# A fused attention and expert kernel on one core: the router summed in PSUM by thirds, even expert capacities, a slot table in four parts

## The chip, the cores and the metric

The kernel runs on one core of a Trainium2 chip. The metric is the time of one execution in microseconds on the device; lower is better. The kernel before takes 606.49 us, the median of three runs (604.68 to 609.28).

## What is computed

Two stages follow each other: windowed attention over 8 batches of 8 heads with 576 positions of width 64, and a mixture of 16 experts (4 groups of 4) over the 4608 tokens that come out of it. Each token goes to one expert, the best of its best group, and its output is weighted by the two softmax values.

```python
# attention: x[token, 512], from windows of 32 keys (half of the heads with a stride of 4)
g_logits = x @ w_group                      # 4 groups
g_idx = argmax(g_logits); g_w = softmax(g_logits)[g_idx]
for g in range(4):
    xg = x[g_idx == g]
    e_logits = xg @ w_expert[g]             # 4 experts in the group
    e_idx = argmax(e_logits); e_w = softmax(e_logits)[e_idx]
    for e in range(4):
        h = maximum(xg[e_idx == e] @ w1[g, e], 0)      # 512 -> 1024
        out[those tokens] = g_w * e_w * (h @ w2[g, e])  # 1024 -> 512
```

## The kernel before

**Attention.** The loop over `s` runs 36 steps of 128 queries and three more that empty its pipeline. A step holds on TensorE (PE): the scores (L266, L278), the transposes of the probabilities of the step before (L301), the product with the values of the step before that (L311), and the transposes of finished rows into `xT` (L363). ScalarE (ACT) takes the exponentials (`p`, L294) and copies out of PSUM; VectorE (DVE) takes the row maxima, differences and normalisation (L288, L289, L339); GpSimd (POOL) shifts the values (L125, L131). Inputs and the finished rows (`xd`) move by DMAs on SyncE's queue.

**Router.** The steps are nine to a pair of batches, 1152 tokens (9 tiles of 128). When a pair is done, `route(bp)` runs beside the attention steps of the next pair: a generator whose pieces are handed out by `spend`, at most 1.8 us of estimated work a step, and which stops for a step where a piece yields 2. So its matmuls over the tokens (L380) stand in one step and the sums of the logits (L391) in the next. The model width of 512 is cut into four row blocks `c`. The first matmuls write block `c` of a third of the tokens to partitions 32c of a PSUM tile, ACT copies each third to `lt` (L387), and nine matmuls against `sumsel` (four stacked unit matrices of 20 columns, L391) add the four blocks and turn the tokens into partitions. DVE then finds group and expert (L396 to L435), matmuls with a triangle of ones count the ranks (L444, L446), and each token gets a slot.

**Slot table.** `tab` holds for every slot of every expert the token, its weight and its row in `xd`. Each 128 tokens multiply a one-hot matrix of the slot's low part (`ohl`, made on ACT, L246 and L247) with `mv`: the one-hot of its high part times the values (`parts`, L502 on DVE; every third tile in the first three routes on POOL, L494 and L495). The three values are split into two fp16 parts each, so `mv` has 6 x 64 columns, multiplied in two matmuls of 192 columns that add into the same PSUM (`tb_ps`, L521). Then `tab` takes the sum (L531), and `select` (L684, L691) and `unpack` (L655 to L657) take an expert's slots out of it.

**Experts.** Expert ranks by size have fixed capacities `CAPS`. Slots past a capacity go through a loop at the end, of no rounds where all fit. Three early pieces of the two largest experts start before routing is done. `layer1` runs 8 x 12 matmuls whose moving side is as wide as the piece (L750), `layer2` 24 matmuls of 512 columns for each tile of 128 rows (L809; a last tile of up to 64 or 32 rows is cut into two or four side by side). Rows come by gathers on POOL (L700) and leave by scatters (L770).

**Order.** In the attention stage PE, ACT, DVE and SyncE take the order of the program as written. After it the string `TAIL` sets by hand how the fourth route, the early pieces and the weights of the second expert alternate. There `R` runs the fourth route up to its first stop, `r` one piece of it.

Of the kernel before, what the change touches and what calls it, by code (L numbers as in the profile page):

```python
# [17 lines left out]
P = 128  # L18
# [15 lines left out]
R256 = 1.5 * 2.0**31  # L34
# [5 lines left out]
CAPS = (448, 408, 368, 304, 304, 304, 296, 288, 272, 264, 256, 256, 248, 240, 216, 192)  # L40
# [17 lines left out]
NCHK = NTOK // P  # L58
NK4 = 4
# [5 lines left out]
def moe_attention_kernel(ctx, tc, q, k, v, cmask, wgate, wpack, out):  # L65
# [89 lines left out]
    wgr = cp.tile([P, 128 + NCHK], F32, name="wgr")  # L155
    wg = wgr[:, 0:128].rearrange("p (c n) -> p c n", c=4)
    sumsel = cp.tile([P, 20], F32, name="sumsel")
# [15 lines left out]
    parts = cp.tile([P, NCHK, 6], F16, name="parts")  # L173
# [9 lines left out]
    def setup(part):  # L183
        if part == 0:
            nc.vector.memset(ones, 1.0)
            nc.gpsimd.affine_select(
                out=upper, in_=ones, pattern=[[1, P]], compare_op=ALU.is_gt, fill=0.0, base=0, channel_multiplier=-1
            )
            nc.sync.dma_start(wgr, wgate)
            nc.vector.tensor_copy(sumsel, id32[:, 0:20])  # L190
            for c in range(1, 4):
                nc.vector.tensor_tensor(sumsel, sumsel, id32[:, 32 * c : 32 * c + 20], ALU.add)
            iota_of(pri, [[-1, 4]], 4, 0)
            iota_of(base[0], [[REG, NE]], 0, 0)
            iota_of(low, [[1, P]], 0, 0)
        if part == 1:
            iota_of(val[:, :, 0], [[P, NCHK]], -NTOK, 1)
            iota_of(parts[:, :, 0], [[P, NCHK]], -NTOK, 0)
            iota_of(parts[:, :, 3], [[0, NCHK]], 0, 1)
# [3 lines left out]
            nc.vector.memset(tab[:, 0], float(NTOK))  # L203
            nc.vector.memset(tab[:, 1], 0.0)
            nc.vector.memset(tab[:, 2], 2.0 * NTOK + 1.0)
            nc.vector.tensor_copy(val[:, :, 2], wgr[:, 128:])
            nc.vector.tensor_scalar(parts[:, :, 2], val[:, :, 2], R256, R256, ALU.add, ALU.subtract)
            nc.vector.tensor_tensor(parts[:, :, 5], val[:, :, 2], parts[:, :, 2], ALU.subtract)
# [161 lines left out]
    def route(bp):  # L370
        lt = sm.tile([P, TPB, P], F32, name="lt")
        TPC = TPB // 3
        for i in range(3):
            ps = (psT, psT, psR)[i].tile([P, TPC * P], F32, name="lt_ps", tag="ttr"[i])
            a0 = i * TPC * P
            cuts = [a0] + [S] * (a0 < S < a0 + TPC * P) + [a0 + TPC * P]
            for a, b in zip(cuts, cuts[1:]):
                bb, s0, n = a // S, a % S, b - a
                for c in range(4):
                    nc.tensor.matmul(  # L380
                        ps[32 * c : 32 * c + 32, a - a0 : b - a0],
                        wg[:, c],
                        xT[bp][:, c, bb, s0 : s0 + n],
                        start=True,
                        stop=True,
                    )
# [88 lines left out]
        nc.vector.reciprocal(val[:, mine, 1], se)  # L475
        yield 0
        nc.vector.tensor_copy(parts[:, mine, 1], val[:, mine, 1])
        yield 0
        nc.vector.tensor_tensor(parts[:, mine, 4], val[:, mine, 1], parts[:, mine, 1], ALU.subtract)
# [4 lines left out]
        for t0 in range(0, n, 3):  # L484
            ohl = sm.tile([P, 3, P], F16, name="ohl", bufs=2)
            mv = sm.tile([P, 3, 6, NE * NK4], F16, name="mv", bufs=2)
            for t in range(3):
# [4 lines left out]
                if last < NBP and t == 2:  # L492
# [4 lines left out]
                        ohh.rearrange("p e k -> p (e k)").unsqueeze(1).broadcast_to([P, 6, NE * NK4]),  # L497
                        parts[:, bp * TPB + t0 + t].unsqueeze(2).broadcast_to([P, 6, NE * NK4]),
# [5 lines left out]
                    high.rearrange("p e k -> p (e k)").unsqueeze(1).broadcast_to([P, 6, NE * NK4]),  # L504
                    hl[:, 1, t0 + t : t0 + t + 1],
                    parts[:, bp * TPB + t0 + t].unsqueeze(2).broadcast_to([P, 6, NE * NK4]),
# [11 lines left out]
            for t1, lo, hv in done:  # L518
                for t in range(3):
                    for h in range(2):  # L520
                        nc.tensor.matmul(  # L521
                            tb_ps,
                            lo[:, t],
                            hv[:, t, 3 * h : 3 * h + 3].rearrange("p v n -> p (v n)"),
                            start=(t1 + t + h == 0),
                            stop=(t1 + t == n - 1 and h == 1),
                        )
# [125 lines left out]
    def unpack(ent, cs, three):  # L653
        n = three.shape[-1]
        nc.vector.tensor_copy(ent[:, 0:3:2, 0:n], three[:, 0:3:2])  # L655
        nc.vector.tensor_scalar(ent[:, 1, 0:n], three[:, 0], 2.0, 0.0, ALU.mult, ALU.add)
        nc.vector.tensor_scalar_mul(cs[:, 0:n], three[:, 1], 1.0 / (SH * SW * SG))  # L657
# [4 lines left out]
    def note_tail(cs, three, cap):  # L662
# [4 lines left out]
        nc.vector.tensor_scalar_add(tq[0:n, 0:1], three[0:n, 0, t : t + 1], -float(NTOK))  # L667
# [446 lines left out]
    with tc.For_i(0, nov, 1) as i:  # L1114
# [11 lines left out]
        nc.vector.tensor_scalar_add(three[:, 0:1], three[:, 0:1], float(NTOK))  # L1126
# [13 lines left out]
def layout(q, k, v, moe_w_group, moe_w_expert, moe_w1, moe_w2):  # L1140
# [37 lines left out]
    wgate = np.concatenate([wgate, 2.0 * (row - NTOK)], axis=1).astype(np.float32)  # L1178
# [26 lines left out]
```

## Time and profile before

| | us |
|---|---|
| median of three runs (lowest to highest) | 606.49 (604.68 to 609.28) |
| the profiled execution | 609.38 |
| its span, first to last instruction | 607.7 |
| busy in the span: PE, PE's weight loads, DVE, ACT, POOL | 571.0, 400.4, 395.1, 329.5, 247.7 |
| mean granted TensorE clock | 0.982 of full |

The profiled execution lies 1.7 us above its span and 2.9 us above the median. Matmuls are pipelined, so PE's busy time counts waits inside the array too. Shares of the whole span mix stages with different limits. A PE clock of 1.00 is 2.4 GHz, one of 0.50 is 1.2 GHz.

### The profile page before, as it was taken

How to read it: one execution, taken by the hardware profiler on the slowest of the kernel's cores; microseconds unless marked ns; L12 is line 12 of the kernel's file. 1: busy time of each engine (PE TensorE's matmuls, PEld its weight loads, DVE VectorE, ACT ScalarE, POOL GpSimd, SP SyncE). 2: the span in 40 equal slices, each digit the busy share in tenths (PEclk: the TensorE clock that was granted, in tenths of full speed). 3: DMA queues.
4: the chain of work that ended last, by engine and by line, in shares of the span. 5: the costliest groups of instructions: out<-in, count | busy, mean ns of one | idle time of the engine just before them, and what ended most of it. 6: DMA issues, size and time to landing. Idle time of an engine off the chain costs nothing.

```text
span 607.7 us, 18716 instructions
## 1 busy us (share of the span) xinstructions
PE 571.0 (94%) x7636; PEld 400.4 (66%) x7636; DVE 395.1 (65%) x800; ACT 329.5 (54%) x658; POOL 247.7 (41%) x314
## 2 busy tenths in 40 slices
PE   5898999988879999999999999999999999999995
PEld 3665776666666668665666575666757767767873
DVE  5764874897957853774778786655755666656720
ACT  2555674675566533774465555465655756656521
POOL 4754582655726324143425151433524413413411
PEclk9999998989989999999999999999999999999999
DMA  7998796799374118676567576757668578677300
GB/s 245 298 287 262 238 277 185 237 356 335 71 250 144 51 47 318 219 259 205 183 198 223 187 229 205 226 175 232 209 211 258 180 243 275 227 233 254 103 30 29
DMA packets 47914, 127.52 MB, mean 210 GB/s; under 512 B 7224, under 2 KB 8126, under 8 KB 47826
## 3 DMA queue, kind: packets, MB, share of 16 engines
q1 hardware_dynamic: 40466, 105.31, 54.9%
q0 software_dynamic: 7360, 20.98, 9.8%
q8 instruction: 62, 1.02, 0.7%
q14 instruction: 26, 0.21, 0.1%
HBM read 107.38 MB, written 19.24 MB: 208 GB/s over the span
## 4 chain that ended last, share of the span: by engine, by line
PE 65%; issue 3%; DVE 2%; POOL 1%; ACT 1%; POOLq 0%
PE y L809 31%; PE a L750 30%; PE pt L731 3%; DVE mv L502 1%; POOL xe L700 1%; PE tb_ps L521 0%; POOL out L770 0%; PE rp L676 0%; ACT off L246 0%; DVE room L758 0%; ACT xT L367 0%; ACT ohl L247 0%; PE o L311 0%; ACT room L757 0%; DVE room L733 0%
## 5 line engine op out<-in xcount | busy, mean ns | idle before, releaser
L700 POOL DMA_INDIRECT xr<-xd,sent x80 | 96.1, 1201 | 35.2 <-issue 22.2
L809 PEld LDWEIGHTS <-hh 128*128 128x128 f16 (+10 forms) x960 | 67.5, 99 | 58.0 <-issue 2.9
L770 POOL DMA_INDIRECT out<-yr,sent x30 | 30.2, 1007 | 180.2 <-ACT yr L783 148.0
L758 DVE SCALAR_TENSOR_TENSOR hl<-a,hh 128x256 f16<-128x256 f32 (+11 forms) x136 | 57.3, 424 | 65.9 <-ACT hh L757 64.8
L757 ACT ACTIVATE hh<-a 128x256 f16<-128x256 f32 (+11 forms) x136 | 51.9, 385 | 51.9 <-PE a L750 51.2
L750 PE MATMUL a<-xh,wb1h 128*128 128x256 f16 (+6 forms) x288 | 77.0, 271 | 0.0
L750 PE MATMUL a<-xl,wb1h 128*128 128x256 f16 (+6 forms) x288 | 77.0, 271 | 0.0
L750 PE MATMUL a<-xh,wb1l 128*128 128x256 f16 (+6 forms) x288 | 77.0, 271 | 0.0
L733 DVE TENSOR_TENSOR xl<-pt,xh 128x512 f16<-128x512 f32 (+10 forms) x42 | 24.8, 594 | 73.5 <-ACT xh L732 73.5
L750 PE MATMUL a<-xh,wa1h 128*128 128x192 f16 (+7 forms) x256 | 71.2, 278 | 0.0
L750 PE MATMUL a<-xh,wa1l 128*128 128x192 f16 (+7 forms) x256 | 71.2, 278 | 0.0
L750 PE MATMUL a<-xl,wa1h 128*128 128x192 f16 (+7 forms) x256 | 71.2, 278 | 0.0
L783 ACT ACTIVATE yr<-y,cs 128x512 f32<-128x512 f32 (+3 forms) x30 | 20.6, 687 | 90.1 <-PE y L809 61.9
L750 PEld LDWEIGHTS <-wa1h 128*128 128x128 f16 x640 | 59.3, 98 | 13.4 <-issue 1.8
L750 PEld LDWEIGHTS <-wb1h 128*128 128x128 f16 x576 | 54.4, 98 | 10.0
L809 PE MATMUL y<-wb2h,hh 128*128 128x512 f16 (+6 forms) x272 | 59.7, 305 | 0.0
L809 PE MATMUL y<-wb2l,hh 128*128 128x512 f16 (+6 forms) x272 | 59.6, 304 | 0.0
L809 PE MATMUL y<-wb2h,hl 128*128 128x512 f16 (+6 forms) x272 | 59.6, 304 | 0.0
L809 PE MATMUL y<-wa2h,hh 128*128 128x512 f16 (+7 forms) x208 | 56.8, 332 | 0.0
L809 PE MATMUL y<-wa2l,hh 128*128 128x512 f16 (+7 forms) x208 | 56.6, 330 | 0.0
L809 PE MATMUL y<-wa2h,hl 128*128 128x512 f16 (+7 forms) x208 | 56.6, 330 | 0.0
L809 PEld LDWEIGHTS <-hl 128*128 128x128 f16 (+10 forms) x480 | 34.6, 99 | 25.2
(190 smaller groups left out, 1255.4 us busy)
## 6 DMA issues: line engine op xcount, KB each, us to landing
w<-wpack SPq DMA_DIRECT2D x128, 512.0 KB, 3.9
vt<-v SPq DMA_DIRECT2D x36, 260.0 KB, 4.8
qb<-q SPq DMA_DIRECT2D x36, 256.0 KB, 4.6
xd<-x SPq DMA_DIRECT2D x72, 128.0 KB, 3.9
kr<-k SPq DMA_DIRECT2D x34, 256.0 KB, 4.4
xr<-xd,sent POOLq DMA_INDIRECT x80, 4.1
kr<-k SPq DMA_DIRECT2D x4, 128.0 KB, 3.2
out<-yr,sent POOLq DMA_INDIRECT x30, 2.8
```

The costliest lines, as they stand in the source:

```text
L502: nc.vector.scalar_tensor_tensor(mv[:, t], high.rearrange("p e k -> p (e k)").unsqueeze(1).broadcast_to([P, 6, NE * NK4]), hl[:, 1, t0 + t ...
L700: nc.gpsimd.indirect_dma_start(out=xr[:, 256 * h : 256 * h + 256], out_offset=None, in_=xd[0:known].rearrange("n (h c) -> (n h) c", h=2), ...
L731: nc.tensor.transpose(pt[:, c, 0:n], xr[0:n, c * P : c * P + P], id32[0:n, 0:n])
L733: nc.vector.tensor_tensor(xl[:, :, t * P : t * P + n], pt[:, :, 0:n], xh[:, :, t * P : t * P + n], ALU.subtract)
L750: nc.tensor.matmul(a[:, 0:cap], ww[:, c * FF + f * P : c * FF + f * P + P], xx[:, c, 0:cap], start=(i == 0), stop=(i == len(mm) - 1),)
L757: nc.scalar.activation(hh[:, f, 0:cap], a[:, 0:cap], AF.Relu)
L758: nc.vector.scalar_tensor_tensor(hl[:, f, 0:cap], a[:, 0:cap], 0.0, hh[:, f, 0:cap], ALU.max, ALU.subtract)
L770: ins = nc.gpsimd.indirect_dma_start(out=out.rearrange("n (g c) -> (n g) c", g=g), out_offset=bass.IndirectOffsetOnAxis(ap=at, axis=0), in ...
L783: nc.scalar.activation(yr[0:n, :], yp[0:n, :], AF.Copy, scale=cs[0:n, t : t + 1])
L809: nc.tensor.matmul(yp[P // g * j : P // g * j + n, 0 : DM // g], h[:, f, t * P : t * P + n], ww[:, f * DM + DM // g * j : f * DM + DM // g ...
```

## The change

**Router.** The thirds of the tokens now lie on partitions 0, 32 and 64 of one PSUM tile, and the four row blocks add up in place: `c` is the outer loop, and only the first matmul of a third has `start`. One copy takes 96 partitions to `lt`. Three matmuls against `sel3` (three unit matrices beside each other, 60 columns) give the logits of nine tiles.

**Slot table.** A token's number and its row are coded as even numbers counted back from the end of its pair of batches, from -2304 to -2, which one fp16 holds; only the weight keeps two parts. `mv` has 4 x 64 columns: one matmul of 192 columns and one of 64 per tile. Since the code of all but the last pair is relative, two new DVE instructions (`sh`) take the pair's offset off the entries that were written.

**Capacities.** `CAPS` sums to 4616 instead of 4664.

```diff
-CAPS = (448, 408, 368, 304, 304, 304, 296, 288, 272, 264, 256, 256, 248, 240, 216, 192)
+CAPS = (442, 406, 368, 302, 300, 298, 292, 284, 266, 264, 256, 256, 242, 238, 214, 188)
...
+PAIR2 = 2 * TPB * P
...
-    parts = cp.tile([P, NCHK, 6], F16, name="parts")
+    parts = cp.tile([P, NCHK, 4], F16, name="parts")
...
     def route(bp):
-        lt = sm.tile([P, TPB, P], F32, name="lt")
         TPC = TPB // 3
-        for i in range(3):
-            ps = (psT, psT, psR)[i].tile([P, TPC * P], F32, name="lt_ps", tag="ttr"[i])
-            a0 = i * TPC * P
-            cuts = [a0] + [S] * (a0 < S < a0 + TPC * P) + [a0 + TPC * P]
-            for a, b in zip(cuts, cuts[1:]):
-                bb, s0, n = a // S, a % S, b - a
-                for c in range(4):
+        lt = sm.tile([3 * 32, TPC * P], F32, name="lt")
+        ps = psT.tile([P, TPC * P], F32, name="lt_ps", tag="t")
+        for c in range(4):
+            for j in range(3):
+                a0, a1 = j * TPC * P, (j + 1) * TPC * P
+                cuts = [a0] + [S] * (a0 < S < a1) + [a1]
+                for a, b in zip(cuts, cuts[1:]):
+                    bb, s0 = a // S, a % S
                     nc.tensor.matmul(
-                        ps[32 * c : 32 * c + 32, a - a0 : b - a0],
+                        ps[32 * j : 32 * j + 32, a - a0 : b - a0],
                         wg[:, c],
-                        xT[bp][:, c, bb, s0 : s0 + n],
-                        start=True,
-                        stop=True,
+                        xT[bp][:, c, bb, s0 : s0 + b - a],
+                        start=(c == 0 and a == a0),
+                        stop=(c == 3 and b == a1),
                     )
-            nc.scalar.copy(lt[:, i * TPC : i * TPC + TPC].rearrange("p t n -> p (t n)"), ps)
+        nc.scalar.copy(lt, ps[0 : 3 * 32])
         yield 2
         lg_ps = psR.tile([P, TPB, 20], F32, name="lg_ps", tag="r")
-        for t in range(TPB):
-            nc.tensor.matmul(lg_ps[:, t], lt[:, t], sumsel, start=True, stop=True)
+        for t in range(TPC):
+            nc.tensor.matmul(
+                lg_ps.rearrange("p (j t) e -> p j t e", t=TPC)[:, :, t],
+                lt[:, t * P : t * P + P],
+                sel3[0 : 3 * 32],
+                start=True,
+                stop=True,
+            )
...
-                    for h in range(2):
+                    for v0, v1 in ((0, 3), (3, 4)):
                         nc.tensor.matmul(
-                            tb_ps,
+                            tb_ps[:, 0 : (v1 - v0) * NE * NK4],
                             lo[:, t],
-                            hv[:, t, 3 * h : 3 * h + 3].rearrange("p v n -> p (v n)"),
...
         tf = tab.rearrange("p v e k -> p (v e k)")
+        if last < NBP:
+            sh = T("sh", [2 * NE * NK4])
+            nc.vector.tensor_scalar(sh, tb_ps[:, NE * NK4 :], 0.0, -float(PAIR2 * (NBP - last)), ALU.is_lt, ALU.mult)
+            yield 0
+            nc.vector.tensor_tensor(tf[:, NE * NK4 :], tf[:, NE * NK4 :], sh, ALU.add)
+            yield 0
         nc.vector.tensor_tensor(tf, tf, tb_ps, ALU.add)
```

The rest follows from the code: set-up instructions for `sel3`, `parts` and `tab`, the order of the three values in `unpack`, `note_tail` and the closing loop, and 36 more columns in the table `wgate` that the host lays out.

On PE, in the attention step after the first pair of batches, this stood ahead of the step's transposes (`lt_ps` are the router's first sums, `tx` the transposes of finished rows, `s` the scores):

```order
L380 MATMUL lt_ps<-xT,wgr 32x384 x4
L380 MATMUL lt_ps<-xT,wgr 32x192 x8
L380 MATMUL lt_ps<-xT,wgr 32x384 x4
L363 MATMUL tx<-id_73,x 128x128 x4
L266 LDWEIGHTS idb
L266 MATMUL s<-masks,idb 128x512
```

and now stands this:

```order
L377 MATMUL lt_ps<-xT,wgr 32x384
L377 MATMUL lt_ps<-xT,wgr 32x192 x2
L377 MATMUL lt_ps<-xT,wgr 32x384 x2
L377 MATMUL lt_ps<-xT,wgr 32x192 x2
L377 MATMUL lt_ps<-xT,wgr 32x384 x2
L377 MATMUL lt_ps<-xT,wgr 32x192 x2
L377 MATMUL lt_ps<-xT,wgr 32x384 x2
L377 MATMUL lt_ps<-xT,wgr 32x192 x2
L377 MATMUL lt_ps<-xT,wgr 32x384
```

Sixteen matmuls stay sixteen, at the same place. Before, four neighbours went to four quarters of the array's columns; now a third of the tokens stays in one quarter for all four blocks, so that three quarters are in use, and the middle third comes in two halves one behind the other.

On PE, one step later, the logits (`lg_ps`) between the product with the values (`o`) and the same transposes, before:

```order
L311 MATMUL o<-vt,pt_122 32x65
L391 MATMUL lg_ps<-sumsel,lt 128x20 x9
L363 MATMUL tx<-id_73,x 128x128 x4
L266 LDWEIGHTS idb
L266 MATMUL s<-masks,idb 128x512
L278 MATMUL s<-kr,qb 32x128 x16
```

and now:

```order
L308 MATMUL o<-vt,pt_122 32x65
L388 MATMUL lg_ps<-sel_155,lt 128x3x20 x3
L360 MATMUL tx<-id_73,x 128x128 x4
L263 LDWEIGHTS idb
L263 MATMUL s<-masks,idb 128x512
L275 MATMUL s<-kr,qb 32x128 x16
```

Nine matmuls became three; what follows them moved up.

On DVE, at the end of the third route, where the second and third early pieces' slots are taken (`room` are an early piece's hidden values, `ente` its rows), before:

```order
L758 SCALAR_TENSOR_TENSOR room<-a,room 128x128 x4
L531 TENSOR_TENSOR tab<-tab,tb_ps 128x192
L684 TENSOR_TENSOR sel_3921<-tab,top 128x48
L691 TENSOR_REDUCE three_3923<-sel_3921 128x3
L655 CAST ente_183<-three_3923 128x2
```

and now:

```order
L767 SCALAR_TENSOR_TENSOR room<-a,room 128x128 x4
L536 TENSOR_SCALAR sh<-tb_ps 128x128
L538 TENSOR_TENSOR tab<-tab,sh 128x128
L540 TENSOR_TENSOR tab<-tab,tb_ps 128x192
L693 TENSOR_TENSOR sel_3897<-tab,top 128x48
L700 TENSOR_REDUCE three_3899<-sel_3897 128x3
```

Two instructions came in ahead of the table's sum, and the selection waits behind them. On POOL, whose order is left to the scheduler there, the second of two clearings of 128x256 (L1079) moved from behind the six gathers of the early pieces to ahead of them, so that the fourth route's softmax sums follow the gathers at once.

## Rows read from the trace of the kernel before

**Rows 1.** The page: its chain by engine, and the DMA share by slices.
```profile
PE 65%; issue 3%; DVE 2%; POOL 1%; ACT 1%; POOLq 0%
...
DMA  7998796799374118676567576757668578677300
```

**Rows 2.** Chain in order of time, expert stage: start us, us, what (304, 288 columns).
```profile
350.44 6.20 PE a L750 x48
...
404.96 5.88 PE a L750 x48
```

**Rows 3.** ACT's timeline: the exponentials of two attention steps, five steps apart.
```profile
28.57 0.63 ACT L294 ACTIVATE p<-d 128x512 f32<-128x512 f32 x1
...
47.43 0.62 ACT L294 ACTIVATE p<-d 128x512 f32<-128x512 f32 x1
```

**Rows 4.** Stretches: us, busy PE PEld DVE ACT POOL, PEclk, DMA share, GB/s.
```profile
54.90:60.60 5.70, 5.55 (x139) 3.47 (x132) 2.27 (x4) 3.69 (x10) 1.93 (x4) 1.00 0.85 245
60.60:66.40 5.80, 5.75 (x133) 4.76 (x132) 4.34 (x11) 2.47 (x8) 1.52 (x6) 1.00 0.71 219
92.90:100.20 7.30, 6.03 (x139) 3.62 (x132) 2.28 (x4) 3.72 (x10) 0.62 (x1) 1.00 0.70 201
100.20:108.20 8.00, 8.00 (x125) 6.40 (x125) 4.31 (x10) 2.30 (x8) 2.87 (x9) 0.58 0.53 150
140.90:146.80 5.90, 5.59 (x140) 3.54 (x132) 3.57 (x5) 4.49 (x11) 2.73 (x3) 1.00 1.03 373
146.80:153.70 6.90, 6.90 (x134) 5.68 (x134) 5.64 (x12) 3.54 (x9) 5.33 (x10) 0.75 0.60 203
```

**Rows 5.** Timeline, third and fourth route: ACT's copies of two thirds, PE's logits.
```profile
142.28 0.48 ACT L387 COPY lt<-lt_ps 128x384 f32<-128x384 f32 x1 [0.17 <-PE lt_ps L380]
...
142.93 0.48 ACT L387 COPY lt<-lt_ps 128x384 f32<-128x384 f32 x1 [0.17 <-PE lt_ps L380]
...
185.76 2.14 PE L391 MATMUL lg_ps<-sumsel,lt 128*128 128x20 f32 x18
```

**Rows 6.** Timeline of DVE: its waits for the logits, and one for the scores.
```profile
59.13 0.69 DVE L288 TENSOR_REDUCE mx<-s 128x8 f32<-128x512 f32 x1 [3.16 <-PE s L278]
...
62.74 0.35 DVE L396 TENSOR_REDUCE mx<-lg_ps 128x45 f32<-128x180 f32 x1 [1.04 <-PE lg_ps L391]
...
102.70 0.35 DVE L396 TENSOR_REDUCE mx<-lg_ps 128x45 f32<-128x180 f32 x1 [1.42 <-PE lg_ps L391]
...
148.75 0.35 DVE L396 TENSOR_REDUCE mx<-lg_ps 128x45 f32<-128x180 f32 x1 [0.86 <-PE lg_ps L391]
```

**Rows 7.** Groups by form, DVE: busy us, mean ns, idle before and its releasers.
```profile
L502 DVE SCALAR_TENSOR_TENSOR mv<-high,hl,parts 128x384 f16<-128x384 f32 x27 | 20.3, 789 | 0.5 <-PE tb_ps L521 0.4
...
L758 DVE SCALAR_TENSOR_TENSOR hl<-a,hh 128x304 f16<-128x304 f32 x24 | 11.2, 469 | 7.4 <-ACT hh L757 7.4
...
L758 DVE SCALAR_TENSOR_TENSOR hl<-a,hh 128x192 f16<-128x192 f32 x16 | 5.7, 356 | 17.3 <-ACT hh L757 17.3
...
L531 DVE TENSOR_TENSOR tab<-tab,tb_ps 128x192 f32<-128x192 f32 x4 | 1.4, 347 | 0.2 <-PE tb_ps L521 0.2
```

**Rows 8.** The tile `mv`: its writers' shortest, median and longest ns.
```profile
L502 DVE SCALAR_TENSOR_TENSOR mv<-high,hl,parts x27: 602/619/1267, 71.7 to 200.8; 128x384 f16<-128x384 f32 x27
L495 POOL TENSOR_TENSOR mv<-ohh,parts x9: 826/829/1193, 71.8 to 176.8; 128x384 f16<-128x384 f32 x9
```

**Rows 9.** Busy time by stretches, where the first expert's weights come in.
```profile
116.00:124.00 8.00, 6.47 (x218) 4.79 (x214) 7.68 (x15) 7.21 (x19) 7.11 (x11) 1.00 0.98 333
```

**Rows 10.** Timeline of the fourth route, and the tile `mv`: who waited for it.
```profile
191.84 0.33 POOL L1079 MEMSET xT<- 128x256 f32 x1
...
194.37 0.22 DVE L475 RECIPROCAL val<-se 128x9 f32<-128x9 f32 x1 [1.27 <-POOL se L428]
...
197.52 0.33 PE L521 MATMUL tb_ps<-mv,ohl 128*128 128x192 f16 x2 [0.40 <-DVE mv L502]
...
  PE tb_ps L521: 1.8, 6
```

More of the change, by code (lines that the diff above doesn't have):

```diff
@@ L189, in setup @@
             nc.sync.dma_start(wgr, wgate)
-            nc.vector.tensor_copy(sumsel, id32[:, 0:20])
-            for c in range(1, 4):
-                nc.vector.tensor_tensor(sumsel, sumsel, id32[:, 32 * c : 32 * c + 20], ALU.add)
+            for j in range(3):
+                nc.vector.tensor_copy(sel3[:, j], id32[:, 32 * j : 32 * j + 20])
             iota_of(pri, [[-1, 4]], 4, 0)
@@ L202, in setup @@
             nc.vector.memset(E16, 0.0)
-            nc.vector.memset(tab[:, 0], float(NTOK))
-            nc.vector.memset(tab[:, 1], 0.0)
+            nc.vector.memset(tab[:, 0], 0.0)
+            nc.vector.memset(tab[:, 1], 2.0 * NTOK)
             nc.vector.memset(tab[:, 2], 2.0 * NTOK + 1.0)
-            nc.vector.tensor_copy(val[:, :, 2], wgr[:, 128:])
-            nc.vector.tensor_scalar(parts[:, :, 2], val[:, :, 2], R256, R256, ALU.add, ALU.subtract)
-            nc.vector.tensor_tensor(parts[:, :, 5], val[:, :, 2], parts[:, :, 2], ALU.subtract)
+            nc.vector.tensor_copy(val[:, :, 2], wgr[:, 128 : 128 + NCHK])
+            nc.vector.tensor_copy(parts[:, :, 2], wgr[:, 128 + NCHK :])
         if part == 2:
@@ L519, in route @@
                 for t in range(3):
-                    for h in range(2):
+                    for v0, v1 in ((0, 3), (3, 4)):
                         nc.tensor.matmul(
-                            tb_ps,
+                            tb_ps[:, 0 : (v1 - v0) * NE * NK4],
                             lo[:, t],
-                            hv[:, t, 3 * h : 3 * h + 3].rearrange("p v n -> p (v n)"),
-                            start=(t1 + t + h == 0),
-                            stop=(t1 + t == n - 1 and h == 1),
+                            hv[:, t, v0:v1].rearrange("p v n -> p (v n)"),
+                            start=(t1 + t + v0 == 0),
+                            stop=(t1 + t == n - 1 and v0 == 3),
                         )
@@ L654, in unpack @@
         n = three.shape[-1]
-        nc.vector.tensor_copy(ent[:, 0:3:2, 0:n], three[:, 0:3:2])
-        nc.vector.tensor_scalar(ent[:, 1, 0:n], three[:, 0], 2.0, 0.0, ALU.mult, ALU.add)
-        nc.vector.tensor_scalar_mul(cs[:, 0:n], three[:, 1], 1.0 / (SH * SW * SG))
+        nc.vector.tensor_copy(ent[:, 1:3, 0:n], three[:, 1:3])
+        nc.vector.tensor_scalar(ent[:, 0, 0:n], three[:, 1], 0.5, 0.0, ALU.mult, ALU.add)
+        nc.vector.tensor_scalar_mul(cs[:, 0:n], three[:, 0], 1.0 / (SH * SW * SG))
     def groups(n):
@@ L666, in note_tail @@
         tq = fs.tile([P, 2], F32, name="tq")
-        nc.vector.tensor_scalar_add(tq[0:n, 0:1], three[0:n, 0, t : t + 1], -float(NTOK))
+        nc.vector.tensor_scalar(tq[0:n, 0:1], three[0:n, 1, t : t + 1], 0.5, -float(NTOK), ALU.mult, ALU.add)
         nc.vector.tensor_copy(tq[0:n, 1:2], cs[0:n, t : t + 1])
@@ L1125, in moe_attention_kernel @@
         nc.vector.tensor_copy(three, three_ps)
-        nc.vector.tensor_scalar_add(three[:, 0:1], three[:, 0:1], float(NTOK))
+        nc.vector.tensor_scalar_add(three[:, 1:2], three[:, 1:2], 2.0 * NTOK)
         nc.vector.tensor_scalar_add(three[:, 2:3], three[:, 2:3], 2.0 * NTOK + 1.0)
@@ L1177, in layout @@
     row = tok // S * S + tok % S % 4 * CLS + tok % S // 4
-    wgate = np.concatenate([wgate, 2.0 * (row - NTOK)], axis=1).astype(np.float32)
+    pair = 2.0 * (row - PAIR2 // 2 * (tok // (PAIR2 // 2) + 1))
+    wgate = np.concatenate([wgate, 2.0 * (row - NTOK), pair], axis=1).astype(np.float32)
     w1 = np.asarray(moe_w1).reshape(NE, 4, P, FF).transpose(0, 2, 1, 3).reshape(NE, P, 4 * FF)
```

27 lines of the change are left out of this document (13 added, 14 removed).

## The prediction

> **What bounds the kernel now.** I read the page's chain first, then the same chain in order of time, then the attention stage by stretches and the engines' timelines there. The page's chain lies on PE for 65% of the span [rows 1]; in order of time it is PE's `layer1` and `layer2` without a gap, so the expert stage costs what its matmuls cost. The reader sees there 48 matmuls of 304 columns in 6.20 us and 48 of 288 in 5.88 us [rows 2]: 0.32 us for 48 x 16 columns, 0.417 ns a column, one column a cycle at 2.4 GHz.
>
> The attention stage ahead of it is a loop whose steps wait on several engines. Five steps without router work take 47.43 - 28.57 = 18.9 us, 3.8 us each [rows 3]; the DMA share there is 0.8 to 0.9 [rows 1], so DMA is the next limit behind PE. The steps that hold the router's matmuls stand out [rows 4]. In pairs, the step of the first sums (`lt`) and that of the logits (`lg`) of routes one to three, they take 5.7 and 5.8 us, 7.3 and 8.0, 5.9 and 6.9. They are 17 us longer together than six plain ones (39.6 against 22.6). PE is busy nearly throughout them, at a granted clock of 0.58 and 0.75 in the `lg` steps of routes two and three against 1.00 in route one's. So what the change does to PE there shows in the time unless DMA or DVE take over.
>
> **The change part by part.** The sum is made in the profiled execution (609.38 us), and the difference carried to the median.
>
> Narrower `layer1`: 48 columns fewer, 96 matmuls to a column: 48 x 96 x 0.417 ns = 1.92 us, all on the chain. No piece changes its number of tiles or groups, so `layer2` stays. The widths of before are multiples of 8; whether 302 or 186 columns cost exactly their count no row shows. If the array rounded up to 8, nothing would be gained. I take -1.9, with 0 to -1.9 as bounds, since all widths seen lie on one line.
>
> Logits: 18 passes (nine matmuls, two passes each) took 2.14 us [rows 5], 119 ns each, for 20 columns; what paces them is the 128 columns of weights, so 60 columns change little. Six passes remain: -1.43 us of PE each route. What then comes late is DVE: it waited for these logits 1.04, 1.42 and 0.86 us [rows 6], and cannot start earlier than its own normalisation ends. So the three steps gain 1.0, 1.4 and, because the DMA share is 1.03 just before the third [rows 4], perhaps 0.6. I take -3.0, between -1.5 (half of it lost to the next wait) and -4.3 (all of PE's gain).
>
> First router sums: two ACT copies of thirds stand 142.93 - 142.28 = 0.65 us apart [rows 5], each third being 384 columns in all four quarters at once: 1.69 ns a column. Before, a quarter streamed 1152 columns (1.95 us); now each of three quarters streams four blocks of 384, 1536 columns (2.60 us): +0.65 us a route. DVE waits for the scores behind this block for 3.16 us [rows 6], so PE decides there, and ACT's two saved copies lie beside PE's work. In route three DMA hides about half: +0.65, +0.65, +0.3 make +1.6. Bounds: 0, if DMA hides all of it, and +2.9, if in each route the second half of the middle third also holds back the last third once, by 192 columns (0.33 us more). That last case is what the Trainium skill's page "TensorE: Matmul & The Clock Gate" (Step-by-step: what each phase is for) speaks for: matmuls stay in program order. By that rule the sum would be 1 us higher; no row here has two neighbours in one quarter with a third matmul behind.
>
> Table matmuls: 9 x 128 columns fewer a route, at most 0.48 us each at 0.417 ns, less if weight loads set the pace, and only partly on the path: -0.3 for the first three routes, bounds 0 and -1.4.
>
> DVE and POOL: DVE's two-input instructions cost 469 ns at 304 columns and 356 at 192 [rows 7], 1.01 ns a column, so each `mv` loses 128 columns, 0.13 us; 18 of the 27 lie in the attention stage: -2.3 us. `sh` adds two instructions of 128 columns; `tab` takes 347 ns for 192 [rows 7], so about 0.28 each, 0.56 a route. In the first two routes that leaves 12 x 0.13 - 1.1 = 0.4 us saved. POOL's `mv` shrinks too, and it delays DVE's where both run (mean 789 ns [rows 7], shortest 602 [rows 8]). DVE is full in route two's table (7.68 of 8.00 us), but so is DMA, with a share of 0.98 [rows 9]. I take -0.9 for the attention stage, bounds -3 and +0.5.
>
> Fourth route: PE's gain there (1.43 - 0.65 = 0.8 us) is hidden, because DVE's `val` waits for POOL's softmax sums, 1.27 us [rows 10], and these queue behind the early pieces' gathers. The gathers start later by the third route's `sh` (+0.56), and one clearing of 0.33 us leaves the path [rows 10]. Behind `val` PE waits for `mv` six times, 1.8 us in all [rows 10], and nine `mv` are 0.13 us shorter each; ACT's copies and DVE's `room` instructions between them give back about half: -0.5. Together -0.3, bounds +0.6 and -1.6.
>
> Clock: the `lg` steps of routes two and three ran at 0.58 and 0.75 and took 2.2 and 1.1 us more than route one's at 1.00 [rows 4], 3.3 us. In both, the logits with their tiny matmuls stood where the clock fell. With two thirds of them gone, dense matmuls follow sooner, and I expect a good half of this back: -1.8. Bounds -3.3 and, if a fall comes in another place, +1.5. The Trainium skill speaks against it: its page "TensorE: Matmul & The Clock Gate" (A second HAM failure mode: psum-queue depth-cycling) has the clock swing where TensorE often idles a little between groups, and a faster PE in a stage paced by DMA idles more. By that rule the term would be 0 or a loss; route one's step, busy 5.75 of 5.80 us at 1.00, agrees with the rule so far.
>
> Sum: -1.9 - 3.0 + 1.6 - 0.3 - 0.9 - 0.3 - 1.8 = -6.6 us. 609.38 becomes 602.8. The profiled execution lies 2.9 us above the median of the three runs, so the median becomes 606.5 - 6.6 = 599.9 us.
>
> **Rivals.** *Swallowed.* The attention stage is paced by DMA (0.8 to 0.9 in plain steps, 1.03 around route three), and what PE and DVE save turns into waits for inputs. Left are `layer1` and the tail: -2.2, 604.3 us. For it speaks the share; against it that the share falls to 0.53 to 0.85 in four of the six router steps [rows 4].
>
> *The clock falls anyway.* Everything but the last term: -4.8, 601.7 us.
>
> *All of it.* The logits give 4.3 and the clock 3.0, DVE 1.5, table and tail 0.6 each, `layer1` 1.9, less 1.9 for the first sums: -10.0, 596.5 us. For it: the router steps are 17 us over plain ones.
>
> *Slower.* Three quarters that add into one PSUM bank do not run side by side. Then 4608 columns stream one after another, 7.8 us a route in place of 1.95: +5.8, three times in the attention stage and about 5 in the fourth route, so 599.9 - 1.6 + 17.5 + 5 = 621 us. It decides from about 2.7 us more a block: three of those take back the other terms of the sum, 8.2 us. Against it: before, four quarters wrote one bank at once at 0.65 us a third.
>
> *A capacity too small.* If the new order of summing moved one token to an expert that is exactly full, a round of the closing loop would come: the weights, 4 MB at 373 GB/s [rows 4], 11 us, and 96 matmuls of 128 columns, 5 us: over 615 us.
>
> **How the numbers follow.** Chances: forecast 0.42, all of it 0.21, swallowed 0.17, clock 0.16, slower 0.03, capacity 0.01. About 1% (6 us) is what a measurement of this kernel can tell from no change; faster by that means under 600.4. That holds for some 0.6 of the forecast's share, nearly all of the best case and a quarter of the clock's: 0.50. Slower is the last two, 0.04; the rest, 0.46, is within 1%. The range leaves out the last two, a piece of the best case below 595.3 and of the swallowed one above 605: 595.3 to 605.0.
>
> **What would show it.** Right: `layer1` of the fourth rank at about 48 x 302 x 0.417 + 0.1 = 6.2 us; the logits in 0.7 us; the first sums in 2.6 to 2.9 us; `lg` steps of 4.5 to 5 us at a clock near 1.00; `mv` at a shortest of 0.47 us. Wrong: first sums of 4 us or more, DVE waits for inputs in place of those for logits, plain steps longer than 3.8 us, or the same falls of the clock.

## The result, and the profile after

The changed kernel takes 601.34 us, the median of 14 runs (598.75 to 604.02), beside 607.39 us for the kernel before on the same chip (14 runs, 604.68 to 614.36). The ratio is 0.9898, with a 95% interval of 0.9875 to 0.9921: 6.05 us faster. The forecast was 6.6 us off a median of 606.5, a ratio of 0.9891.

The two profiled executions make the change look larger than it is: 609.38 us before (2.0 above its median), 598.75 after (the fastest of its 14). So the rows below show where time went, and the medians how much.

| | before | after |
|---|---|---|
| median, us | 607.39 | 601.34 |
| profiled execution, us (span) | 609.38 (607.7) | 598.75 (597.0) |
| expert stage, from the `y` group ahead of the first 96 `layer1` matmuls to the last `y` of the chain, us | 204.73 to 585.14: 380.4 | 196.51 to 574.80: 378.3 |
| last pass of the fourth route's logits to the start of that stage, us | 187.90 to 204.73: 16.8 | 179.75 to 196.51: 16.8 |
| first sums of the fourth route to the start of that stage, us | 182.33 to 204.73: 22.4 | 174.81 to 196.51: 21.7 |
| first sums of the fourth route, us | 182.33 to 184.48: 2.15 | 174.81 to 177.61: 2.79 |

The page of after, its chain by engine and the DMA share by slices; they answer to [rows 1]:

```profile
PE 67%; issue 3%; DVE 2%; ACT 1%; POOL 0%; POOLq 0%; ACTq 0%
...
DMA  7998797898473227885677576756867578777300
```

PE still carries the chain, and DMA is no fuller. The chain in order of time (start us, us, what), where [rows 2] had 6.20 us for 304 columns and 5.88 for 288:

```profile
286.77 6.16 PE a L759 x48
...
314.11 6.12 PE a L759 x48
...
341.38 6.08 PE a L759 x48
...
395.48 5.80 PE a L759 x48
```

These are 302, 300, 298 and 284 columns. Widths that are no multiple of 8 lie on the same line: 4 columns from the first to the third take 0.08 us, 48 x 4 x 0.417 ns.

The six route steps by stretches (us, busy PE, PEld, DVE, ACT, POOL, then PEclk, DMA share, GB/s), each from one step's exponentials to the next step's, as in [rows 4]:

```profile
55.50:62.30 6.80, 6.41 (x140) 4.25 (x134) 2.28 (x4) 2.69 (x8) 1.86 (x3) 1.00 0.66 199
62.30:67.00 4.70, 4.70 (x126) 3.69 (x124) 4.25 (x11) 2.70 (x8) 1.60 (x6) 1.00 0.77 219
93.60:99.60 6.00, 6.00 (x140) 4.40 (x134) 2.28 (x4) 2.74 (x7) 1.86 (x3) 1.00 0.68 219
99.60:104.30 4.70, 4.70 (x126) 3.68 (x124) 4.25 (x11) 2.70 (x8) 1.54 (x6) 1.00 0.86 258
136.40:141.50 5.10, 5.03 (x120) 3.24 (x119) 3.31 (x5) 3.55 (x8) 2.93 (x3) 1.00 1.02 362
141.50:147.80 6.30, 6.03 (x158) 4.69 (x157) 5.89 (x12) 3.45 (x8) 4.42 (x6) 1.00 0.78 246
```

33.6 us in place of 39.6, all at a granted clock of 1.00; the `lg` steps of routes two and three had 0.58 and 0.75. What stays in them is PE: it is busy nearly throughout. Of the 6.0 us, 5.0 lie in the `lg` steps, and the `lt` steps are 1.0 us shorter too, although their block of first sums is longer. (In route three the first sums start at 134.47 us, 2.0 us ahead of their stretch, in a step of 5.27 us where 5.16 stood before.) One reason shows in the kernel before: there PE paused inside the first sums of route two (timeline), for nothing that the profile names, and after it does not.

```profile
94.45 1.80 PE L380 MATMUL lt_ps<-xT,wgr 128*32 128x384 f32 x25 [0.93 <-issue]
```

The six plain steps between routes one and two take 23.4 us in both profiles. The five of [rows 3] take 20.0 us after (28.01 to 48.02) in place of 18.9, but they lie ahead of all router work.

The timelines of ACT and PE in the fourth route (start us, us, engine, line, operation, in brackets the wait before it):

```profile
177.67 0.48 ACT L384 COPY lt<-lt_ps 96x384 f32<-96x384 f32 x1 [2.81 <-PE lt_ps L377]
...
178.91 0.83 PE L388 MATMUL lg_ps<-sel,lt 96*128 96x60 f32 x6
179.58 0.60 PE L818 MATMUL y<-wa2h,room 128*128 128x512 f16 x2
```

One ACT copy takes the place of three ([rows 5]), and the next matmul starts 0.67 us after the first of six logit passes, 0.11 us a pass; DVE's three waits for logits [rows 6] are gone from its list of waits.

The tile `mv`, its writers' shortest, median and longest ns and who waited for it, and the start of the fourth route's table on DVE ([rows 8, 10]):

```profile
L505 DVE SCALAR_TENSOR_TENSOR mv<-high,hl,parts x27: 474/486/926, 72.3 to 192.8; 128x256 f16<-128x256 f32 x27
L498 POOL TENSOR_TENSOR mv<-ohh,parts x9: 607/616/845, 72.4 to 169.6; 128x256 f16<-128x256 f32 x9
...
  PE tb_ps L524: 1.0, 3
...
187.12 0.22 DVE L478 RECIPROCAL val<-se 128x9 f32<-128x9 f32 x1 [0.89 <-POOL se L431]
```

Each `mv` is 0.13 us shorter on DVE and 0.21 on POOL, PE waits for three of them in place of six, and `val` still waits for POOL's sums, for less time. Those sums read ACT's `df`. The timelines of ACT and POOL, first before and then after:

```profile
189.24 0.35 ACT L419 ACTIVATE df<-df 128x180 f32<-128x180 f32 x1 [1.56 <-DVE oh L402]
192.12 0.35 POOL L422 TENSOR_TENSOR df<-df 128x90 f32<-128x90 f32 x1
...
182.40 0.35 ACT L422 ACTIVATE df<-df 128x180 f32<-128x180 f32 x1 [1.56 <-DVE oh L405]
184.85 0.35 POOL L425 TENSOR_TENSOR df<-df 128x90 f32<-128x90 f32 x1
```

In both, `df` is ready over 2 us before POOL takes it up, and POOL does so at once when its gathers (and, before, the clearing) are done.

### The profile page after: what moved, and what is told of

It is laid out like the page before. It is cut to its first block, busy times and chain, and to the rows that moved or that the text cites. A ratio compares the mean times of both kernels' runs of the same rounds, so it can differ in the third digit from the quotient of the medians.

```text
span 597.0 us, 18617 instructions
## 1 busy us (share of the span) xinstructions
PE 561.4 (94%) x7588; PEld 393.8 (66%) x7588; DVE 389.5 (65%) x804; ACT 326.4 (55%) x650; POOL 241.9 (41%) x313
## 3 DMA queue, kind: packets, MB, share of 16 engines
q0 software_dynamic: 7760, 20.99, 10.2%
## 4 chain that ended last, share of the span: by engine, by line
PE 67%; issue 3%; DVE 2%; ACT 1%; POOL 0%; POOLq 0%; ACTq 0%
PE y L818 32%; PE a L759 31%; PE pt L740 3%; DVE mv L505 1%; PE lt_ps L377 0%; PE tx L360 0%; PE o L308 0%; POOL out L779 0%; PE rp L685 0%; PE tb_ps L524 0%; DVE wb1l L641 0%; PE t L298 0%; ACT wb1h L644 0%; ACT room L766 0%; ACT off L243 0%
## 5 line engine op out<-in xcount | busy, mean ns | idle before, releaser
L818 PEld LDWEIGHTS <-hh 128*128 128x128 f16 (+14 forms) x960 | 67.3, 99 | 57.6 <-issue 2.5
L759 PE MATMUL a<-xh,wb1h 128*128 128x256 f16 (+7 forms) x288 | 76.6, 270 | 0.0
L759 PE MATMUL a<-xh,wb1l 128*128 128x256 f16 (+7 forms) x288 | 76.5, 269 | 0.0
L759 PE MATMUL a<-xl,wb1h 128*128 128x256 f16 (+7 forms) x288 | 76.5, 269 | 0.0
L759 PE MATMUL a<-xh,wa1h 128*128 128x186 f16 (+7 forms) x256 | 70.8, 277 | 0.0
L759 PE MATMUL a<-xl,wa1h 128*128 128x186 f16 (+7 forms) x256 | 70.7, 277 | 0.0
L759 PE MATMUL a<-xh,wa1l 128*128 128x186 f16 (+7 forms) x256 | 70.7, 277 | 0.0
L759 PEld LDWEIGHTS <-wa1h 128*128 128x128 f16 x640 | 59.0, 98 | 11.5 <-issue 0.3
L818 PE MATMUL y<-wb2h,hh 128*128 128x512 f16 (+7 forms) x272 | 59.7, 305 | 0.0
L818 PE MATMUL y<-wb2l,hh 128*128 128x512 f16 (+7 forms) x272 | 59.5, 304 | 0.0
L818 PE MATMUL y<-wb2h,hl 128*128 128x512 f16 (+7 forms) x272 | 59.5, 304 | 0.0
```

Source lines behind the costliest of these rows:

```text
L759: nc.tensor.matmul(a[:, 0:cap], ww[:, c * FF + f * P : c * FF + f * P + P], xx[:, c, 0:cap], start=(i == 0), stop=(i == len(mm) - 1),)
L818: nc.tensor.matmul(yp[P // g * j : P // g * j + n, 0 : DM // g], h[:, f, t * P : t * P + n], ww[:, f * DM + DM // g * j : f * DM + DM // g ...
```

## Experiments

They ran on two further chips, the first four on one, the rest on the other; the kernel before takes 625 us on the one and 622 to 623 on the other. Each ratio below is to the kernel before on the chip of that batch. That these chips are slower, and how, turned out to matter; it stands with the capacities.

**The parts alone.** Three kernels, each the kernel before with one part of the change; and the changed kernel with more logits. *The capacities:*

```diff
-CAPS = (448, 408, 368, 304, 304, 304, 296, 288, 272, 264, 256, 256, 248, 240, 216, 192)
+CAPS = (442, 406, 368, 302, 300, 298, 292, 284, 266, 264, 256, 256, 242, 238, 214, 188)
```

> The kernel before with the new capacities alone. Forecast: layer1 streams 48 columns less, 96 matmuls each at 0.417 ns: 1.9 us under before (0.997), and 48 matmuls of 302 columns take 6.16 us in the chain against 6.20 for 304. Rival (widths cost as if rounded up to 8): 0 us, and 302 columns cost 6.20 us.

Measured: 618.74 us (6 runs), ratio 0.990 (0.9856 to 0.9944): 6.0 us faster, three times the columns' price. 48 matmuls of 302 columns take 6.16 us here too.

*The router:* the kernel before with `route`'s new sums and `sel3`.

```diff
-        for i in range(3):
-            ps = (psT, psT, psR)[i].tile([P, TPC * P], F32, name="lt_ps", tag="ttr"[i])
...
-        for t in range(TPB):
-            nc.tensor.matmul(lg_ps[:, t], lt[:, t], sumsel, start=True, stop=True)
+        ps = psT.tile([P, TPC * P], F32, name="lt_ps", tag="t")
+        for c in range(4):
+            for j in range(3):
...
+        for t in range(TPC):
```

> The kernel before with the new router alone. Forecast: first sums 2.7 us in place of 2.1, logits 0.7 in place of 2.1, lg steps of 4.7 us at a clock of 1.00; together -1.4 us from the matmuls and -1.8 from the clock, 3.2 us under before (0.995). Rival (the clock falls anyway): 1.4 us under. Rival (swallowed by DMA): 0 us, with plain steps longer than 3.8 us.

Measured: 620.31 us (12 runs), 0.9925 (0.9894 to 0.9955): 4.7 us faster by the ratio. The forecast of 3.2 us lies in the interval (2.8 to 6.6 us), the rivals' 1.4 and 0 do not. Its `lg` steps take 4.67, 4.67 and 6.09 us, all at a clock of 1.00.

*The table:* the changed kernel with the capacities and `route`'s sums of before, which leaves the table in four parts.

> The kernel before with the slot table in four parts alone, sh included. Forecast: 1.5 us under before (0.9975), mv at a shortest of 474 ns. Rival (DVE's gain is hidden by DMA and given back by sh): 0 us.

Measured: 622.88 us (12 runs), 0.9977 (0.9944 to 1.0009): 1.4 us faster by the ratio, as expected, but no change lies in its interval too.

*Logits three times*, each logit matmul of the changed kernel issued three times into the same place:

```diff
-        for t in range(TPC):
+        for t in [t for t in range(TPC) for _ in range(3)]:
```

> The changed kernel with each of the three logit matmuls issued three times in a row (18 passes again, same values). Forecast: the logits take 2.1 us again, DVE waits for them some 1 us in each lg step, and the gain of the logits and the clock goes: 3.0 to 4.8 us over the changed kernel, 0.995 to 0.998 of before; if the clock term is real, the granted clock falls below 0.8 in one or two of the lg steps. Rival (swallowed): within 1 us of the changed kernel, 0.990.

Measured: 620.74 us (12 runs), 0.9936 (0.9901 to 0.9971). Its 18 passes take 2.22 us in place of 0.88, and DVE waits for them again, as this kernel's tile `lg_ps` shows (shortest, median, longest ns; below, who waited):

```profile
L388 PE MATMUL lg_ps<-sel,lt x72: 272/275/320, 62.9 to 187.6; 96*128 96x60 f32 x72
...
  DVE mx L399: 2.5, 3
```

One part of the expectation was a miss: the granted clock was to fall below 0.8 in one or two `lg` steps if the clock term was real, and it is 1.00 in all three (columns as above):

```profile
63.21:68.82 5.61, 5.61 (x136) 4.83 (x136) 4.34 (x11) 2.46 (x8) 1.57 (x6) 1.00 0.71 220
102.82:108.42 5.60, 5.60 (x136) 4.82 (x135) 4.34 (x11) 2.49 (x8) 1.54 (x6) 1.00 0.75 217
145.03:152.63 7.60, 6.99 (x162) 5.73 (x164) 6.34 (x12) 3.49 (x9) 5.82 (x9) 1.00 0.85 298
```

These steps take 4.67, 4.67 and 6.08 us in the changed kernel's first control below (on the other of the two chips), also at 1.00. So the passes cost some 0.9, 0.9 and 1.5 us with no fall of the clock, and their number alone did not bring one here. The expectation took the changed kernel at 0.990; that kernel was then run on such a chip, and stands at 0.984.

**The whole beside them.** The changed kernel once more, as a control, and with the old capacities:

> The changed kernel once more, beside its parts on one chip. My theory: the chip on which the parts ran alone adds a cost of its own in the expert stage, and the whole change is worth there about what it was worth before: ratio 0.990 (0.988 to 0.993). Rival: the parts add up as measured alone on that chip (0.990, 0.9925 and 0.998), and the whole comes to 0.981 or less.

Measured: 610.70 us (6 runs), 0.9841 (0.9788 to 0.9894); a second control in the next batch gave 612.74 us (6 runs), 0.9834 (0.9801 to 0.9867).

> The changed kernel as a control, beside the three that follow. The whole change gave 0.9898 on the first chip and 0.9841 on the second; both theories of the next runs allow 0.984 to 0.990, which says on which kind of chip the batch runs. On the second kind the expert stage takes about 385.7 us from its first y group to its last, with about 4.8 us of issue gaps on PE; on the first kind 378.3 us with none.

So my theory of a chip-independent 0.990 fell: the second control's interval leaves it out. The parts do add up on chips of this kind, within their intervals: by the medians 6.0 + 4.4 + 1.9 = 12.3 us alone on the one, 11.5 and 10.4 us together on the other. Tripled logits cost 0.0095 of 622 us over the first control, 5.9 us; the two kernels ran on different chips, and their intervals together allow 2 to 10 us.

> The changed kernel with the capacities of before. My theory: 48 columns in 96 matmuls each come back, 1.9 us: 0.3% slower than the changed kernel, a ratio to the kernel before of about 0.993. Rival: the capacities are worth what they gave alone, 6 us: the ratio then comes to 0.998 to 1.000, and the expert stage between its first y matmul and the end grows by over 4 us.

Measured: 618.23 us (12 runs), 0.9949 (0.9916 to 0.9982), 6.7 to 7.5 us slower than the changed kernel by the ratio or the medians. Both expectations counted from 0.990; from the control's 0.984 the theory comes to 0.987 and the rival to 0.994, so the rival holds. The expert stage shows where: from its first `y` group to its last on the chain, us, with PE's waits there that the view of waits calls "issue":

| kernel | capacities | expert stage | issue | start of the stage |
|---|---|---|---|---|
| before, first chip | old | 380.4 | 0 | 204.7 |
| changed, first chip | new | 378.3 | 0 | 196.5 |
| table alone | old | 390.9 | 6.3 | 210.5 |
| router alone | old | 391.1 | 6.3 | 203.5 |
| capacities undone | old | 390.9 | 5.7 | 202.6 |
| capacities alone | new | 385.2 | 4.0 | 209.8 |
| logits thrice | new | 385.7 | 4.7 | 210.6 |
| changed, two controls | new | 385.7, 385.2 | 4.4, 4.3 | 203.4, 204.1 |

The stage also starts later on these chips: from the last pass of the fourth route's logits it takes 21.5 to 23.5 us in their rows of the table, against 16.8 in both of the first chip. And PE has gaps of up to 1 us in the middle of runs of matmuls, which the first chip's two profiles lack. With the old capacities most of the difference falls into one place, behind the late piece of the first rank. There the chain of the kernel with the capacities undone reads (start us, us, what):

```profile
237.79 0.88 PE y L818 x13
238.67 0.55 issue
239.22 0.42 PE y L818 x4
239.64 0.33 issue
239.97 0.27 PE y L818
240.25 0.44 issue
240.68 0.42 PE y L818 x4
241.10 1.02 issue
242.12 0.30 PE y L818 x2
242.42 0.76 PE pt L740 x4
```

and that of the changed kernel on the same chip:

```profile
241.41 1.08 PE y L818 x5
242.49 0.36 issue
242.85 1.67 PE y L818 x7
```

2.3 us of gaps stand there in place of 0.4, one to four `y` matmuls come at a time between them, and the clock falls after them. The stretches show it (columns as above), first of the capacities undone:

```profile
236.00:254.00 18.00, 15.67 (x141) 10.47 (x139) 5.89 (x11) 8.04 (x15) 6.04 (x6) 0.91 0.55 195
```

and of the changed kernel:

```profile
236.00:254.00 18.00, 17.64 (x213) 14.11 (x211) 9.32 (x18) 10.48 (x21) 6.60 (x7) 1.00 0.70 249
```

All three kernels with the full old set have this fall there (0.91 to 0.92), none with the new set has it, and the kernel before on the first chip has not; that is one profile of each kernel. I then asked whether the first capacity alone brings it: the changed kernel with 448 in place of 442,

> The changed kernel with only the first capacity as before (448 in place of 442, so its late piece has 192 rows and not 186). Theory (one place): the three long issue gaps on PE in the y matmuls behind this piece, and the fall of the clock after them, come from how its matmuls meet PE's supply of instructions there; on a chip with such gaps this alone costs 3 to 4 us (expert stage 389 us, clock 0.91 around 236 to 254 us). Rival (columns only): 6 columns x 96 x 0.417 ns = 0.24 us, and the stretch stays at a clock of 1.00. On a chip without gaps both say 0.24 us.

and the kernel before with only 442:

> The kernel before with only the first capacity changed (442). Theory (one place): on a chip with gaps it gives 3 to 4 us of the 6 that all the capacities gave alone, a ratio of 0.994, with no fall of the clock behind that piece. Rival (columns only): 0.2 us, a ratio of 1.000, and the fall stays.

Measured: 613.30 us (6 runs), 0.9856 (0.9819 to 0.9894), 0.6 us slower than the control beside it, with an expert stage of 385.6 us and a clock of 1.00 in that stretch: a miss. And 617.93 us (11 runs), 0.9914 (0.988 to 0.9947), 5.2 us faster than the kernel before, with an expert stage of 386.7 us and no fall: a hit. So six columns in one rank give most of what all the capacities give on these chips, but putting them back alone does not take it away. The price is that of one unlucky stretch of the old kernel, not of the columns. What arms the stretch (the exact widths ahead of it, or when its instructions arrive) stays open.

**The first sums.** First doubled (the second time over the first), to ask whether PE or DMA sets the pace of the attention stage:

```diff
-        for c in range(4):
+        for c in [0, 1, 2, 3] * 2:
             for j in range(3):
```

> The changed kernel with the matmuls of the first router sums issued twice, the second time over the first: 2.6 us more of PE a route. My theory: PE sets the pace of these steps, so routes one and two pay in full, route three half, the fourth nothing: +6.5 us over the changed kernel (5 to 8). Rival (swallowed): DMA paces the attention stage, and it costs under 3 us.

Measured: 622.86 us (12 runs), 1.0011 (0.9975 to 1.0046): 12 us over the changed kernel. The stretch from first to last of the block in route two (us, busy times, PEclk, DMA share, GB/s) of this kernel:

```profile
97.99:103.38 5.39, 5.39 (x73) 4.07 (x65) 0.90 (x2) 0.70 (x2) 1.86 (x3) 1.00 0.63 177
```

and of the changed kernel, the first control:

```profile
93.10:95.89 2.79, 2.79 (x39) 1.92 (x33) 1.07 (x3) 0.77 (x2) 0.68 (x2) 1.00 0.92 265
```

2.60 us more a block, as computed, and four blocks make 10.4 us. The total alone does not tell who pays (the two intervals allow 7 to 15 us), but the steps do, in the two profiles: the two steps of route one take 2.9 us more than in the control, those of route two 2.5, those of route three 4.3 (there with a clock of 0.88 in the first), and from the fourth route's first sums to the expert stage it takes 28.8 us in place of 26.7. So no route hides them, on this chip. DMA takes none of it back, and its share falls while PE works.

Then with the two loops exchanged, so that neighbours in program order write the same quarter:

```diff
-        for c in range(4):
-            for j in range(3):
+        for j in range(3):
+            for c in range(4):
```

> The changed kernel with the loops of the first router sums exchanged: all four blocks of one third, then the next third, so that neighbours in the order write the same quarter of the columns. Theory: matmuls run beside each other only where neighbours lie in different quarters, so the block takes 4608 columns one after another, 7.8 us in place of 2.79, and the kernel loses 15 to 20 us in four routes. Rival: the quarters run beside each other whatever the order, the block stays under 3.5 us and the time within 2 us.

Measured: 624.33 us (12 runs), 1.0029 (1.0002 to 1.0055): 11.6 us over the control by the medians. The block of the fourth route as a stretch of this kernel:

```profile
185.99:192.06 6.07, 6.07 (x36) 2.90 (x35) 2.67 (x14) 0.05 (x1) 3.44 (x4) 1.00 0.56 204
```

6.07 us is neither the 7.8 of one stream nor the 2.79 of quarters that never wait for each other: both expectations miss. Four blocks of 3.28 us more make 13.1 us. What lies between shows in PE's groups by form in three stretches of that block (186.1 to 187.2, 187.35 to 188.2, 188.65 to 189.2; form, count of records, two to a matmul):

```profile
L377 PE MATMUL lt_ps<-xT,wgr 128*32 128x384 f32 x4 | 1.5, 492 | 0.0
...
L377 PE MATMUL lt_ps<-xT,wgr 128*32 128x384 f32 x4 | 1.5, 486 | 0.0
L377 PE MATMUL lt_ps<-xT,wgr 128*32 128x192 f32 x6 | 1.2, 330 | 0.0
...
L377 PE MATMUL lt_ps<-xT,wgr 128*32 128x192 f32 x5 | 1.0, 326 | 0.0
L377 PE MATMUL lt_ps<-xT,wgr 128*32 128x384 f32 x1 | 0.5, 486 | 0.0
```

The program has four matmuls of 384 columns, eight of 192, four of 384. At first the first third runs alone; in the second stretch the middle third's 192 columns run beside it although the first third is not through its queue (in the trace the first pass of 192 starts at 187.31 us, three of the first third's eight passes at 187.62, 187.95 and 188.27); and at the end of the middle third the last third starts before it has ended. So a matmul to another quarter starts ahead of matmuls that stand before it in the program. The changed kernel shows the same in its own order: in its first 0.35 us of the fourth route's block (after, 174.8 to 175.15) stand the first passes of the first and of the last third and two passes of 192 columns, which are those of the middle third's first half.

```profile
L377 PE MATMUL lt_ps<-xT,wgr 128*32 128x384 f32 x2 | 0.5, 510 | 0.0
L377 PE MATMUL lt_ps<-xT,wgr 128*32 128x192 f32 x2 | 0.5, 338 | 0.0
```

The middle third's second half stands ahead of the last third in the program, and starts 0.34 us behind it in the trace (175.17 and 174.83 us).

**A candidate.** The fourth route's logits ahead of the second slice of expert weights in the written order:

```diff
-    "R0w0wr0rrrrrrrrrrr1rrrr0rr1r1rr1r1rr1rrB1w12w1ww112w2w2w2w2O2O2O2O2O2O"
+    "R0w0rw0rrrrrrrrrrr1rrrr0rr1r1rr1r1rr1rrB1w12w1ww112w2w2w2w2O2O2O2O2O2O"
```

> The changed kernel with the fourth route's logits piece ahead of the second slice of the expert weights in the written order, so that DVE's maximum over the logits no longer stands behind the scaling of a weight slice (1.2 us). My theory: the chain from the logits to the ranks sets when the expert stage starts, 0.5 to 1 us faster than the changed kernel. Rival: the wait for POOL's sums takes up the gain, no difference (within 0.3 us).

Measured: 613.98 us (6 runs), 0.9876 (0.9832 to 0.9921): no gain over the control's 0.9841, and the point lies on the slower side. DVE's timeline of this kernel says why not:

```profile
185.27 0.29 DVE L767 SCALAR_TENSOR_TENSOR room<-a,room 128x128 f16<-128x128 f32 x1 [1.93 <-issue]
187.13 0.35 DVE L399 TENSOR_REDUCE mx<-lg_ps 128x45 f32<-128x180 f32 x1 [1.57 <-remote]
187.39 1.22 DVE L641 SCALAR_TENSOR_TENSOR wb1l<-w,wb1h 128x1024 f16<-128x1024 f32 x1
```

The maximum now stands ahead of the slice's 1.22 us, as meant, but it starts 4.6 us after the last logit pass (182.53 us) in place of 4.8 in the control (181.67, 186.50): `room` and the maximum itself stall ahead of it, for a releaser that the profile does not name. On the first chip, where the maximum follows the logits by 1.5 us (179.75, 181.26), it was not tried.

## Why the prediction was right, and which terms were not

The forecast ratio 0.9891 lies in the measured interval, and the capacities and the router paid on their own too. But the total agrees better than its terms: two were mis-sized, and the clock's came without the reason that was given for it. The two profiles are 10.6 us apart where the medians are 6.05, so they show where the terms lie, and not their exact sizes.

**Narrower `layer1` (-1.9).** Right on the chip it was made for: 302 columns take 6.16 us where 6.2 was said, and the expert stage is 2.1 us shorter. On no chip do widths cost as if rounded up to 8. On the other two chips the same edit is worth 6 to 7.5 us, by a stall that no row of before could show, since the first chip does not have it.

**Logits (-3.0).** The mechanism is shown: 0.67 us a route, DVE's waits gone, and route one's `lg` step, at a clock of 1.00 before and after, 1.1 us shorter where 1.0 was said. Putting the passes back gives 0.9, 0.9 and 1.5 us back in the three steps, again at 1.00.

**Clock (-1.8).** The effect is there, the reason is not shown. The `lg` steps of routes two and three run at 1.00, and the three steps together give 5.0 us where logits and clock were to give 4.8. But "with two thirds of them gone, dense matmuls follow sooner" would have the fall come back with 18 passes, and with tripled logits it did not. Three steps are few: in the four kernels with the old router the clock falls in six of twelve `lg` steps (0.58 to 0.76), in the nine with six passes in none of 27. So the falls went with the old router; what in it brings them stays open. Nor is the size known. Over 45 to 200 us of each profile the granted clock is 0.93 to 0.95, mean 0.94, in the five kernels with 18 logit passes, and 0.93 to 0.98, mean 0.96, in the nine with six: the ranges overlap, and the falls left the `lg` steps but not the stage (after, the stretch from 120 to 130 us is at 0.83). The rule that the prediction took from the Trainium skill's page "TensorE: Matmul & The Clock Gate" (A second HAM failure mode: psum-queue depth-cycling), by which nothing was to be gained, does not show in these steps.

**First sums (+1.6).** The block was right to 0.01 us (2.15 to 2.79, +0.64; said: +0.65). The extra 1 us did not come. The Trainium skill's page "TensorE: Matmul & The Clock Gate" (Step-by-step: what each phase is for) has matmuls stay in program order. The measurement differs: matmuls of different quarters overtake, in the changed kernel (174.83 against 175.17 us) and with the loops exchanged. But as a term of the time +1.6 was wrong, twice. Half hidden in route three does not hold: doubled sums cost that route no less than the others. And on the first chip the `lt` steps became 1.0 us shorter, not 1.6 longer: PE's pause of 0.93 us in route two's block went away, which no term had. All five kernels with 18 logit passes have it there (0.4 to 0.9 us), none of the nine with six; its cause was not found, nor that of the rest.

**Fourth route (-0.3).** On the first chip the path was the one that the prediction named, and the term was too small. POOL's sums start behind the gathers in both profiles, 2.5 and 2.1 us after ACT's `df` is ready (189.59 to 192.12 us, 182.75 to 184.85), so PE's 1.31 us on the logits (2.14 to 0.83) is hidden there, as said. Counted from the fourth route's first sums, the first gather comes 0.4 us later (said: 0.56), from it to `val` 10.2 us become 10.0, and from `val` to the expert stage 10.4 become 9.4, where 0.5 was said for the shorter `mv`: together -0.7 us. That the table has 16.8 us twice is then chance. On the other two chips the path is another: in all twelve profiles there POOL's sums wait for ACT's `df` (0.4 to 4.9 us), which starts from the logits, and doubled first sums cost that route 2.1 us.

**Table, DVE and POOL (-0.3 and -0.9).** `mv` at 0.474 us (said: 0.47), `sh` as said (its sum in `tab` is 294 ns, `tab` 354). The part alone gave 1.4 us (-0.6 to 3.5), the forecast with the tail's -0.3 was 1.5; the interval is too wide to call it shown.

**The rivals.** *Swallowed* falls: 2.2 us lies outside the interval of the ratio (4.8 to 7.6 us), the router steps are 6.0 us shorter, and doubled sums paid in full while the DMA share fell to 0.63. (Against it the prediction counted four of six router steps at a share of 0.53 to 0.85; [rows 4] has five.) *Slower* falls: the block takes 2.79 us, and even in turn 6.07. *A capacity too small* did not come. *All of it*, 596.5 us, is under every run. *The clock falls anyway* (601.7 us) has the number nearest to 601.34, but its condition is not met, since the `lg` steps run at 1.00; with the median of before now at 607.39, the forecast's -6.6 stands at 600.8 and this rival's -4.8 at 602.6, and the runs do not separate the two numbers.

## What to carry to other kernels

Where a stage's steps seem paced by one engine, double the suspected work once, and read the steps as well as the total: they tell which of them pay. That less work saves as much as more work costs is a further step: the `lt` steps got more work and still became shorter. Before a wait counts as hiding something, look at what its releaser was waiting for, on each chip: POOL's sums stood behind gathers on one chip and behind the logits on two others. When an effect comes as forecast, test its reason too: the clock rose, but not for the reason given. And measure a small gain on more than one chip: six columns were worth 0.2 us by their count and 5 us on a chip with a stall.

## What the runs showed that I had not expected

- Matmuls that write different quarters of the columns overtake, in the changed kernel's own order too: in turn, a pass of the next third started with three of the eight passes before it not yet started, and the block took 6.07 us in place of 7.8.
- Two chips have gaps of up to 1.0 us in PE's matmul runs of the expert stage, 3.8 to 6.3 us in all, where the waits view names no releaser; some recur at the same place in the program (27 or 28 matmuls into one group of 48, for one). The first chip's profiles have none. The cause was not found.
- A set of tile widths can be unlucky: 2.3 to 2.6 us of such gaps and a fall of the clock to 0.91 or 0.92 over 18 us, which none of the three other sets of widths tried shows.
